# Three feed-forward steps summed pair by pair during the attention, window masks in strided selections, some early loads on ScalarE's queue, and a new order

## The chip, the core and the metric

The kernel runs on one core of a Trainium2 chip. A core has five engines with their own instruction queues: TensorE (PE in the profile, with PEld for its weight loads), VectorE (DVE), ScalarE (ACT), GpSimd (POOL) and SyncE (SP), which here only issues loads and stores. The engines meet through semaphores. The metric is the time of one execution on the device in microseconds (us), lower is better.

## The reference, cut to what matters

Eight batches, eight heads, 512 local and 32 global tokens, head size 64. Local queries see the 32 globals and a band of 32 tokens to either side; global queries see everything. The concatenated heads of all 4352 rows then go through a feed-forward block without bias.

```python
s_ll = np.where(np.abs(pos[:, None] - pos[None, :]) <= 32, s_ll, -1000000000.0)
out_l = np.matmul(sm(np.concatenate([s_lg, s_ll], axis=-1)), np.concatenate([v_g, v_l], axis=2))
out_g = np.matmul(sm(s_g), v_all)
x = np.ascontiguousarray(attn_out.transpose(0, 2, 1, 3)).reshape(B * S, H * D)
h = x @ w_in            # 4352 x 512 by 512 x 2048
return ((h - np.tanh(h)) @ w_out).astype(np.float32)
```

## The kernel before, in words

Everything is written as operations (class `Order`): each has a function that issues its instructions, the engines that may do it with their costs, the keys that it reads and writes, a due time, and for TensorE the PSUM banks that it needs. When the kernel is built, `Order.run` plays them through as a list schedule and writes the instructions of each engine in the order that comes out. The tables `CFG`, `NUDGE`, `CHOICE` and `HOLD` are the numbers that shift due times, engine preferences and starts, so they alone set the order; on the chip each engine then works its list strictly from front to back.

The work has three stretches. First, batch 0's attention in four head pairs (class `Pair`): transposes of keys and queries, scores, softmax (smallest value on VectorE, exponential on ScalarE, normalising on GpSimd), transposes of the probabilities, and the product with the values (L824). In this stretch TensorE has gaps, which are filled with matmuls on a mask that nobody reads (`fill`, L1943). Meanwhile the weights arrive as 64-bit numbers, of which the load brings all bytes; ScalarE (`rebias`, L525), VectorE (`low` L529, `join` L533) make them float32, and they are split into a high part (`high`, L446) and a remainder (`rest`, L539, on GpSimd). The activations x are split likewise into x_hi and x_lo (L446, L835).

Second, for batches 1 to 7 attention in windows (class `WindowPair`), between which TensorE does the feed-forward block of the batch before (class `Chunk`): 16 steps, each with a sum h of 12 matmuls of 512 columns (three products high-high, high-low, low-high times four blocks of d_model, one block per head pair, L1290), then tanh on ScalarE (L1298), h - tanh on VectorE (L1301), its high part ghi (L446) and remainder glo (L1307), and 12 matmuls with w_out into four accumulator banks (L1338). A step's sum can begin only when all four head pairs of the batch are done, since `add_hidden` takes one product over all four blocks as one operation. `add_window_masks` writes the masks of the windows on GpSimd, block by block. Third, the tail: the last batch's feed-forward block with combined products (L1660, L1686, L1780).

The first pair of the windows is interleaved with the end of batch 0's attention: its scores (L960, L976) and the smallest values of its windows on VectorE (L1053, "window peaks" below) come before x of the last head pair is finished. All loads but two are issued by SyncE.

## Time and profile before

| | |
|---|---|
| time, median of 3 runs | 906.06 us (904.59 to 906.87) |
| the profiled execution | 903.53 us, its span 901.6 us |
| TensorE busy | 883.5 us, 98% of the span |
| VectorE, ScalarE, GpSimd busy | 643.9, 405.9, 319.9 us |
| granted TensorE clock | 0.999 of full speed, the 2.4 GHz level |
| first and last matmul | 5.23 us, 897 us |

Read it with two cautions. Busy time of TensorE is from start to modelled end of pipelined matmuls, so 98% says that it is hardly ever without work, not that it is at its peak. And the average hides that the first 65 us are another regime than the rest, which is why the rows below come from stretches.

### The profile page before, as it was taken

The numbers are of one execution on the slowest core, as the hardware profiler recorded it, in microseconds if no ns is written. First come the engines' busy times: TensorE is split into PE (matmuls) and PEld (weight loads), VectorE is DVE, ScalarE is ACT, GpSimd is POOL, SyncE is SP. The second block draws the span as 40 slices with busy tenths as digits, with TensorE's granted clock in tenths as the row PEclk, the third lists the DMA queues.
The fourth block names the chain that finished last, engine by engine and source line by source line (L and its number), as shares of the span: only waits on it lengthen the run. The fifth ranks groups of instructions, "written<-read, shape, count | busy, mean of one in ns | idle before, by whom it ended". The sixth has DMA issues, their size and how long they took to land.

```text
span 901.6 us, 21546 instructions
## 1 busy us (share of the span) xinstructions
PE 883.5 (98%) x7664; PEld 730.2 (81%) x7664; DVE 643.9 (71%) x2309; ACT 405.9 (45%) x1192; POOL 319.9 (35%) x525
## 2 busy tenths in 40 slices
PE   6889999999999999999999999999999999999998
PEld 4668888888888888888888888888888888899886
DVE  6997767877777557857777557857777658787662
ACT  6986665534344334423444343423444343443332
POOL 7767765333333323333333323323333323000000
PEclk9999999999999999999999999999999999999999
DMA  9768746533334223423334223423334110100001
GB/s 224 173 182 221 185 104 139 124 72 65 66 65 113 45 54 67 96 61 64 66 65 113 46 51 73 95 61 62 65 70 108 43 31 13 47 0 1 1 1 71
DMA packets 266059, 72.20 MB, mean 80 GB/s; under 512 B 250593, under 2 KB 259297, under 8 KB 265953
## 3 DMA queue, kind: packets, MB, share of 16 engines
q1 hardware_dynamic: 264752, 70.44, 34.5%
q8 instruction: 61, 1.00, 0.4%
q10 hardware_dynamic: 1200, 0.39, 0.2%
q14 instruction: 46, 0.37, 0.1%
HBM read 61.87 MB, written 8.91 MB: 79 GB/s over the span
## 4 chain that ended last, share of the span: by engine, by line
PE 91%; DVE 2%; DMA 2%; ACT 1%; POOL 1%; SPq 1%; issue 1%; POOLq 0%; ACTq 0%; DVEq 0%
PE bank L1338 34%; PE bank L1290 32%; PE bank L1660 7%; PE bank L1147 6%; PE bank L1780 6%; PE bank L960 3%; PE bank L976 1%; PE bank L1686 1%; DVE keys_first L1092 1%; DMA stage<-in_moe_w_out_dram 1%; DMA values<-in_v_g_dram 0%; DMA wpair<-in_moe_w_out_dram 0%; ACT prob L1237 0%; ACT t L1237 0%; DMA first_q<-in_moe_w_in_dram 0%
## 5 line engine op out<-in xcount | busy, mean ns | idle before, releaser
L1307 POOL TENSOR_TENSOR glo<-t,ghi 128x512 fp32r<-128x512 f32 x112 | 146.1, 1304 | 291.3 <-PE bank L1338 233.5
L1092 DVE STREAM_TRANSPOSE keys_first<-prob 32x256 f32<-32x256 f32 x384 | 167.3, 436 | 10.6 <-POOL prob L1074 3.5
L1298 ACT ACTIVATE t<-bank 128x512 f32<-128x512 f32 x112 | 66.7, 596 | 179.7 <-PE bank L1290 175.9
L1301 DVE TENSOR_TENSOR t<-bank,t 128x512 f32<-128x512 f32 x112 | 76.6, 684 | 80.0 <-ACT t L1298 78.4
L1338 PE MATMUL bank<-w_out_lo,ghi 128*128 128x512 f32 x448 | 124.9, 393 | 0.0
L1338 PE MATMUL bank<-w_out_hi,ghi 128*128 128x512 f32 x448 | 124.1, 391 | 0.4 <-ACT ghi L446 0.4
L1338 PE MATMUL bank<-w_out_hi,glo 128*128 128x512 f32 x448 | 124.2, 391 | 0.0
L1290 PE MATMUL bank<-x_lo,w_in_hi 128*128 128x512 f32 x448 | 120.2, 390 | 1.3 <-DVE x_lo L835 1.3
L1290 PE MATMUL bank<-x_hi,w_in_hi 128*128 128x512 f32 x448 | 120.8, 392 | 0.4 <-ACT x_hi L446 0.4
L446 ACT CAST ghi<-t 128x512 fp32r<-128x512 f32 (+1 forms) x118 | 72.5, 614 | 107.3 <-PE bank L1338 82.7
L1290 PE MATMUL bank<-x_hi,w_in_lo 128*128 128x512 f32 x448 | 119.8, 389 | 0.0
L1074 POOL TENSOR_SCALAR prob<-prob,st 128x128 f32<-128x128 f32 x224 | 80.6, 378 | 109.0 <-DVE st L456 79.5
L1053 DVE CUSTOM_DVE_ANT_0 prob<-bank,wraw 128x128 f32<-128x128 f32 x224 | 53.7, 287 | 82.3 <-PE bank L960 81.5
L1290 PEld LDWEIGHTS bank<-x_lo,w_in_hi 128*128 128x128 f32 x448 | 84.1, 188 | 19.3 <-DVE x_lo L835 1.7
L1338 PEld LDWEIGHTS bank<-w_out_hi,ghi 128*128 128x128 f32 x448 | 83.9, 188 | 19.6 <-issue 1.8
L1338 PEld LDWEIGHTS bank<-w_out_lo,ghi 128*128 128x128 f32 x448 | 83.0, 188 | 20.4 <-issue 4.0
L1290 PEld LDWEIGHTS bank<-x_hi,w_in_hi 128*128 128x128 f32 x448 | 83.3, 188 | 19.6 <-DVE st L1053 1.2
L1338 PEld LDWEIGHTS bank<-w_out_hi,glo 128*128 128x128 f32 x448 | 83.5, 188 | 19.4 <-issue 2.4
L1290 PEld LDWEIGHTS bank<-x_hi,w_in_lo 128*128 128x128 f32 x448 | 84.1, 188 | 17.6
L1061 ACT ACTIVATE prob<-prob,st 128x128 f32<-128x128 f32 x224 | 87.9, 401 | 1.0 <-DVE st L1053 0.2
L446 ACT CAST x_hi<-bank 128x256 fp32r<-128x256 f32 x62 | 20.6, 375 | 86.1 <-PE bank L976 84.3
L1147 PEld LDWEIGHTS bank<-keys_first,values 128*64 128x64 f32 x784 | 49.3, 138 | 10.3 <-DVE t L1301 5.6
(230 smaller groups left out, 1373.4 us busy)
## 6 DMA issues: line engine op xcount, KB each, us to landing
rawkq<-in_q_l_dram SPq DMA_DIRECT2D x112, 64.0 KB, 2.2
rawkq<-in_k_l_dram SPq DMA_DIRECT2D x112, 64.0 KB, 2.4
out_dram<-wpair SPq DMA_DIRECT2D x28, 256.0 KB, 2.3
values<-in_v_l_dram SPq DMA_DIRECT2D x28, 120.0 KB, 2.3
keys_first<-in_v_l_dram SPq DMA_DIRECT2D x28, 120.0 KB, 2.7
stage<-in_moe_w_out_dram SPq DMA_DIRECT2D x6, 512.0 KB, 4.4
wpair<-in_moe_w_out_dram SPq DMA_DIRECT2D x6, 512.0 KB, 5.4
first_q<-in_moe_w_in_dram SPq DMA_DIRECT2D x6, 512.0 KB, 4.8
```

Source lines behind the costliest of these rows:

```text
L446: (nc.scalar.copy if e == "A" else nc.vector.tensor_copy)(dst, src)
L1061: nc.scalar.activation(x, x, AF.Exp, bias=s[:, k:k + 1], scale=-1.0, accum_out=s[:, 8 + k:9 + k])
L1074: nc.gpsimd.tensor_scalar(x, x, s[:, k:k + 1], 1.0, op0=ALU.mult, op1=ALU.mult)
L1092: nc.vector.transpose(view(win_kf[W * k:W * k + W], [(CH, 2), (P, NT), (1, W)], 3 * G + W * i), src)
L1147: nc.tensor.matmul(dst, win_values[h][:, window(b)], src, start=n == 0, stop=n == len(parts) - 1, skip_group_check=True)
L1290: nc.tensor.matmul(self.h[s][:, j * n:(j + 1) * n], w[:, cc, f * P:(f + 1) * P], self.x()[xi][:, cc, :n], start=part == 0 and cc == 0 and ...
L1298: nc.scalar.activation(tt_[q], self.h[s], AF.Tanh)
L1301: nc.vector.tensor_sub(tt_[q], self.h.pop(s), tt_[q])
L1307: eng[e].tensor_sub(gg[q][1], tt_[q], f32(gg[q][0]))
L1338: nc.tensor.matmul(self.acc[tt], g[:, j * self.n + tt * P:j * self.n + (tt + 1) * P], low_out(f) if wi else high_out(f), start=s == 0 and ...
L1660: nc.tensor.matmul(self.hold(tt, tags), g(), low_out(f) if wi else high_out(f), start=first and k < len(tts), stop=last and k == len(mms) - 1)
L1780: nc.tensor.matmul(dst[:, at], w, m, start=fresh and n == 1, stop=n == 6, skip_group_check=True)
```

## The change

Three things in the code, and the tables that set the order.

The first three steps of batch 0's feed-forward block (`AHEAD = 3`) no longer have their sum as three operations over all four blocks of d_model but as four operations over one block each (`column`: three matmuls). A block's operation reads only the x of its own head pair. The first two of these sums sit in banks of the accumulator pool. The window masks come in two operations of strided selections over up to five blocks at once instead of four with one selection per block. And loads of weights, of the raw keys and queries after the first pair, and of batch 0's values may be issued by SyncE or ScalarE, whichever the list schedule finds earlier with a penalty. `CFG`, `NUDGE`, `CHOICE` and `HOLD` are new throughout; of the tables a few lines stand for all.

```diff
@@ -297,6 +297,7 @@
+    AHEAD = 3
...
-    CFG = dict(win=1940.613, a_g=0.0342, a_kg=0.1721, a_ph=0.0237, a_qs=1.4715, a_w=0.0254, a_wn=0.1779, a_xg=7.3446, d_g=0.274,
+    CFG = dict(win=-1646.8252, a_g=0.121, a_kg=0.1264, a_ph=0.1183, a_qs=3.1154, a_w=0.0917, a_wn=0.0597, a_xg=7.3446, d_g=82.3869,
...
@@ -454,6 +465,12 @@
     def add_epsilon(x, to, y):
         nc.vector.tensor_reduce(out=y, in_=view(x, [(1, x.shape[1]), (to, 2)]), axis=mybir.AxisListType.X, op=ALU.add)
         nc.vector.reciprocal(x, y)
+
+    def queue(e):
+        return nc.scalar if e == "A" else nc.sync
+
+    def queues(d):
+        return [("S", d), ("A", d + 0.15, CFG["a_ld"])]

     def either(n, kind, psum=False):

@@ -515,7 +532,7 @@
         def load(e, _):
             if WIDE:
                 box["v"] = raw[:, :, 0]
-                nc.sync.dma_start(raw.bitcast(I32).rearrange("p (a c) k -> p a (c k)", a=a), src)
+                queue(e).dma_start(raw.bitcast(I32).rearrange("p (a c) k -> p a (c k)", a=a), src)
             else:
                 box["v"] = raw.rearrange("p n k -> p (n k)")[:, :N]
                 nc.sync.dma_start(box["v"].rearrange("p (a c) -> p a c", a=a), src)
@@ -539,7 +556,7 @@
             eng[e].tensor_sub(lo(), box["v"].rearrange("p (a c) -> p a c", a=a), f32(hi()))

         own = [("w", kind, f, i, p) for i in ((j,) if half else (0, 1)) for p in range(2)]
-        add(("S", 0.37), load, due, w=keys, res=spare, xfer=0.9 * N / 256)
+        add(queues(0.37), load, due, w=keys, res=spare, xfer=0.9 * N / 256)
         if WIDE:
             add(("A", (N + 300) / 1200), rebias, due, r=keys, w=keys)
             add(("D", (N / 2 + 146) / 960), low, due, r=keys, w=keys, lock=True)
@@ -614,12 +631,12 @@
             def load(a, src):
                 def fn(e, _):
                     for h in range(2):
-                        (nc.scalar if h and self.j == 0 else nc.sync).dma_start(first_raw[self.set][:, a, :, h],
+                        (nc.scalar if h and self.j == 0 else queue(e)).dma_start(first_raw[self.set][:, a, :, h],
                                                                              src[self.b, 2 * self.jj + h].rearrange("(t p) d -> p t d", p=P))
                 return fn

             for a in range(2):
-                add(("S", 0.95), load(a, (k_l, q_l)[a]), self.due(self.C["o_ld"] - 8), w=[self.key[a]], xfer=1.3)
+                add(queues(0.95) if self.j else ("S", 0.95), load(a, (k_l, q_l)[a]), self.due(self.C["o_ld"] - 8), w=[self.key[a]], xfer=1.3)

         def add_turn(self):
             rk, rq, pw, pk, pq = self.key
@@ -854,22 +871,23 @@
         return k + k // 3

     def add_window_masks():
-        def mask(j):
+        def blocks(i, c, n, step):
+            return view(win_m()[W * i:W * i + W], [(step, n), (1, W)], c)
+
+        places = {-1: ((0, P, 3, P), (1, 0, 4, P), (2, 0, 4, P), (3, 0, 3, P), (3, 3 * P + W, 1, P)),
+                  1: ((0, W, 3, 160), (0, 480, 1, P), (1, 64, 2, 160), (1, 352, 2, 96), (2, 96, 2, P), (2, 320, 2, 160), (3, 96, 1, P), (3, 192, 2, 160))}
+
+        def mask(s):
             def fn(e, _):
-                m = win_mask(j)
-                nc.gpsimd.memset(m, 0.0)
-                for i in range(4):
-                    rows, b = slice(W * i, W * i + W), 4 * j + i
-                    for n in range(3):
-                        k = window(b) + n
-                        c = W * (pos(k) - pos(window(b)))
-                        x = m[rows, c:c + W]
-                        if abs(k - b) > 1:
-                            nc.gpsimd.memset(x, BIG)
-                        elif k != b:
-                            s = k - b
-                            nc.gpsimd.affine_select(out=x, in_=x, pattern=[[-s, W]], base=0, channel_multiplier=s,
-                                                    compare_op=ALU.is_ge, fill=BIG)
+                if s < 0:
+                    nc.gpsimd.memset(win_m()[:, :S], 0.0)
+                for p in places[s]:
+                    x = blocks(*p)
+                    nc.gpsimd.affine_select(out=x, in_=x, pattern=[[0, p[2]], [-s, W]], base=0, channel_multiplier=s,
+                                            compare_op=ALU.is_ge, fill=BIG)
+                if s > 0:
+                    nc.gpsimd.memset(win_m()[:W, 2 * W:3 * W], BIG)
+                    nc.gpsimd.memset(win_m()[3 * W:, 3 * P:3 * P + W], BIG)
             return fn

         def ends(e, _):
@@ -878,8 +896,8 @@
                 nc.vector.memset(win_gmask()[W * rows:W * rows + W, W * lo:W * hi], BIG)

         due = base(H) - 300
-        for j in range(NT):
-            add(("P", 1.85), mask(j), due + j, w=["gm"], )
+        for x in (-1, 1):
+            add(("P", 2.15), mask(x), due + x, w=["gm"])
         add(("D", 0.77), ends, due, w=["gm"])

     def add_globals(b):
@@ -1249,11 +1267,11 @@

                 src = v_l[self.b, self.h]
                 for a in range(2):
-                    nc.sync.dma_start(raw[:96, 3 * a:3 * a + 3], bass.AP(src.tensor, src.offset + 224 * D * a, [[D, 96], [96 * D, 3], [1, D]]))
+                    queue(e).dma_start(raw[:96, 3 * a:3 * a + 3], bass.AP(src.tensor, src.offset + 224 * D * a, [[D, 96], [96 * D, 3], [1, D]]))
                 g = v_g[self.b, self.h]
-                nc.sync.dma_start(raw[96:], bass.AP(g.tensor, g.offset, [[D, G], [0, 6], [1, D]]))
-
-            add(("S", 1.45), load, self.pair.due(self.C["o_vl"] + self.C["o_tw"] * self.two), w=[f"vh{self.two}"], xfer=0.95)
+                queue(e).dma_start(raw[96:], bass.AP(g.tensor, g.offset, [[D, G], [0, 6], [1, D]]))
+
+            add(queues(1.45), load, self.pair.due(self.C["o_vl"] + self.C["o_tw"] * self.two), w=[f"vh{self.two}"], xfer=0.95)


     step_no = [0]
@@ -1308,7 +1326,23 @@

             self.g[s] = gg[q]
             fs = range(s * self.per, (s + 1) * self.per)
-            for part in range(3):
+            early = s < AHEAD and self.name == "b0"
+
+            def column(cc):
+                def fn(e, tags):
+                    if cc == 0:
+                        self.h[s] = bank([P, 512], tags[hk])
+                    for wi, xi in ((0, 0), (0, 1), (1, 0)):
+                        nc.tensor.matmul(self.h[s], (w_in_hi, w_in_lo)[wi][:, cc, s * P:(s + 1) * P], self.x()[xi][:, cc, :n],
+                                         start=cc == 0 and wi + xi == 0, stop=cc == NCC - 1 and wi == 1)
+                return fn
+
+            for cc in range(NCC * early):
+                r = [k + (xi,) for k in self.xkeys if k[2] // 2 == cc for xi in range(2)] + [("w", "i", s, j, wi) for j in range(2) for wi in range(2)]
+                last = cc == NCC - 1
+                add(("T", 0.68), column(cc), due + 0.1 * cc - CFG["ahead"] * (not last), r=r, w=[hk],
+                    res=[tk] if last else (), alloc=[(hk, "acc" if s < 2 else "h")] if cc == 0 else ())
+            for part in range(3 * (not early)):
                 wi, xi = ((0, 0), (0, 1), (1, 0))[part]
                 r = [k + (xi,) for k in self.xkeys] + [("w", "i", f, j, wi) for f in fs for j in range(2)]
                 add(("T", 0.907), mm(part), due + 0.1 * part, r=r, w=[hk],
```

What stands in the engines' lists shows it best. In the rows below a line number is that of the kernel before or of the changed kernel, `bank_96` to `bank_103` are the eight PSUM banks, and xN means that a row stands N times.

TensorE, before: behind batch 0's last product with the values the fillers come, of which the first row here is the last, then the sums of steps 0 and 1 (24 matmuls), then the transposes of the first windows (the first shown), and after those the first w_out products (L1338).

```order
L1943 MATMUL bank_96<-mask_88 128x224
L1290 MATMUL bank_96<-x_hi_85,w_in_hi 128x512 x4
L1290 MATMUL bank_99<-x_hi_85,w_in_hi 128x512 x4
L1290 MATMUL bank_99<-x_lo_86,w_in_hi 128x512 x4
L1290 MATMUL bank_99<-x_hi_85,w_in_lo 128x512 x4
L1290 MATMUL bank_96<-x_lo_86,w_in_hi 128x512 x4
L1290 MATMUL bank_96<-x_hi_85,w_in_lo 128x512 x4
L1114 MATMUL bank_98<-idr,prob 128x64
```

TensorE, changed, the same place from the second half of that last product on: L1336 is a `column`, one block of one step.

```order
L841 MATMUL bank_102<-keys_first,values 64x128 x2
L841 MATMUL bank_102<-keys_first,values 64x64 x2
L841 MATMUL bank_102<-keys_first,values 64x160 x2
L1336 MATMUL bank_96<-x_hi_85,w_in_hi 128x512
L1336 MATMUL bank_96<-x_lo_86,w_in_hi 128x512
L1336 MATMUL bank_96<-x_hi_85,w_in_lo 128x512
L1336 MATMUL bank_100<-x_hi_85,w_in_hi 128x512
L1336 MATMUL bank_100<-x_lo_86,w_in_hi 128x512
L1336 MATMUL bank_100<-x_hi_85,w_in_lo 128x512
L1336 MATMUL bank_103<-x_hi_85,w_in_hi 128x512
L1336 MATMUL bank_103<-x_lo_86,w_in_hi 128x512
L1336 MATMUL bank_103<-x_hi_85,w_in_lo 128x512
```

What moved: 27 of the 36 matmuls of steps 0 to 2 need only x of the first three pairs and stand between the products and transposes of the attention from the second pair on (the last three of them are the first three L1336 here); 9 need the last pair's x, of which the 6 here come before the window transposes and the first w_out products (L1372), and 3 of step 2 behind the first eight of those. The sums of steps 1 and 0 lie in `bank_100` and `bank_103`, which the w_out products take over as accumulators. Before the first w_out product stand 33 matmuls of feed-forward sums instead of 24, and 69 fillers instead of 78. Behind it the numbers of matmuls are equal in each kind, apart from these 9.

VectorE, before, behind the first window peaks (L1053, the row ahead of these); the next rows are the two x_lo of the last pair (L835).

```order
L450 TENSOR_REDUCE st_91<-st_91 32x2 x3
L533 SCALAR_TENSOR_TENSOR stage<-stage 128x512
L455 TENSOR_REDUCE st_91<-st_91 128x4
L456 RECIPROCAL st_91<-st_91 128x4
L533 SCALAR_TENSOR_TENSOR first_kw_63<-first_kw_63 128x256
L1005 TENSOR_REDUCE st_91<-st_91 32x2
L940 STREAM_TRANSPOSE hi_104<-rawkq 128x512
L455 TENSOR_REDUCE st_91<-st_91 128x4
L456 RECIPROCAL st_91<-st_91 128x4
L933 STREAM_TRANSPOSE first_m<-rawkq 128x5x96
L934 STREAM_TRANSPOSE first_m<-rawkq 128x32
L450 TENSOR_REDUCE st_91<-st_91 32x2 x3
```

VectorE, changed, the same place: the last window peaks (L1071) stand ahead, L852 is x_lo.

```order
L461 TENSOR_REDUCE st_91<-st_91 32x2 x3
L466 TENSOR_REDUCE st_91<-st_91 128x4
L467 RECIPROCAL st_91<-st_91 128x4
L1023 TENSOR_REDUCE st_91<-st_91 32x2
L546 TENSOR_SCALAR stage<-stage 128x512
L958 STREAM_TRANSPOSE hi_104<-rawkq 128x512
L852 TENSOR_TENSOR x_lo_86<-bank_101,x_hi_85 128x256
L856 COPY xg<-bank_101 128x32
L466 TENSOR_REDUCE st_91<-st_91 128x4
L467 RECIPROCAL st_91<-st_91 128x4
L461 TENSOR_REDUCE st_91<-st_91 32x2 x3
L852 TENSOR_TENSOR x_lo_86<-bank_102,x_hi_85 128x256
```

What moved: the transposes into `first_m` now stand among the peaks, and two `join` operations on weights, one of 512 and one of 256 columns, are gone from between the peaks and x_lo: the smaller stands earlier, the larger weight's comes later. From the first window peak to the second x_lo the lists have else the same instructions. In the stretch up to the first window peak VectorE has six more: one more w_out_hi cast, one more x_hi cast, two more copies of `first_g`, two more `join` of 256 columns, one more `low` of 256 and one fewer of 512; a 512-column copy of `first_q` less and one of `keys_first` more cancel.

ScalarE, before, from its start (L446 is a copy, L525 `rebias`, L676 and L677 the global exponentials).

```order
L617 DMA first_raw<-in_k_l_dram 128x4x64
L617 DMA first_raw<-in_q_l_dram 128x4x64
L446 ACT_TABLE_LOAD
L446 COPY first_g<-bank_96 128x128
L446 COPY first_m<-bank_96 64x4x32 x2
L446 COPY first_kw<-first_g 128x2x2x32
L446 COPY first_kw<-bank_97 128x2x96
L446 COPY first_kw<-bank_97 128x2x192
L446 COPY first_kw<-first_g 128x2x2x32
L525 ACTIVATE stage<-stage 128x512
L676 ACTIVATE pg<-pg,st_91 64x32
L677 ACTIVATE pg,st_91<-pg,st_91 64x576
```

ScalarE, changed, from its start (L1255 is the exponential of a window of scores).

```order
L634 DMA first_raw<-in_k_l_dram 128x4x64
L634 DMA first_raw<-in_q_l_dram 128x4x64
L535 DMA stage<-in_moe_w_out_dram 128x1024
L634 DMA first_raw<-in_k_l_dram 128x4x64 x2
L457 ACT_TABLE_LOAD
L457 COPY first_g<-bank_96 128x128
L457 COPY first_m<-bank_96 64x4x32 x2
L457 COPY first_kw<-first_g 128x2x2x32
L1270 DMA values<-in_v_l_dram 96x3x64 x2
L1272 DMA values<-in_v_g_dram 32x6x64
L1255 ACTIVATE t_68,st_91<-t_68,st_91 128x224 x2
L1255 ACTIVATE prob,st_91<-prob,st_91 128x224 x2
```

What moved: six of the first stretch's loads go from SyncE to ScalarE, three at its start and three ahead of its first exponential, each of these three behind a semaphore of an earlier load; the first `rebias` goes behind the first eight exponentials. Eight more loads, of weights, stand on ScalarE behind the first w_out product, most behind a semaphore of GpSimd, which has to be done with the buffer. On GpSimd the two instructions of the identity now stand ahead of the three of one of the first masks, and the window masks are 13 selections and 3 fills instead of 30 and 6.

## Rows read from the trace of the kernel before

**Rows 1.** The page: busy time and share of the span of each engine.

```profile
PE 883.5 (98%) x7664; PEld 730.2 (81%) x7664; DVE 643.9 (71%) x2309; ACT 405.9 (45%) x1192; POOL 319.9 (35%) x525
```

**Rows 2.** Stretches (start:end length, busy us and instructions of each engine, clock, DMA share, GB/s).

```profile
5.23:52.70 47.47, 41.38 (x507) 30.85 (x507) 41.47 (x168) 42.14 (x137) 34.04 (x82) 1.00 0.87 207
52.70:65.48 12.78, 10.34 (x87) 8.01 (x88) 12.32 (x57) 9.86 (x34) 8.89 (x13) 1.00 0.67 179
65.48:897.40 831.92, 831.74 (x7070) 691.37 (x7070) 588.82 (x2073) 352.29 (x1023) 272.85 (x412) 1.00 0.31 70
```

**Rows 3.** Timeline of TensorE: start, length, what [idle before <- releaser].

```profile
5.23 0.68 PE L579 MATMUL bank<-idr,first_kw 64*128 64x64 f32 x4 [5.23 <-DVE idr L1384]
...
55.05 1.61 PE L1943 MATMUL bank<-mask 128*128 128x224 bf16 x15
...
65.48 1.20 PE L1338 MATMUL bank<-w_out_hi,ghi 128*128 128x512 f32 x4 [0.38 <-ACT ghi L446]
...
68.33 1.07 PE L1338 MATMUL bank<-w_out_hi,glo 128*128 128x512 f32 x4
```

**Rows 4.** Chain that ended last, in order of time: start, length, what.

```profile
31.66 4.47 DMA values<-in_v_g_dram
...
64.17 0.61 DVE t L1301
...
64.81 0.63 ACT ghi L446
```

**Rows 5.** Timeline of VectorE at the end of the first attention.

```profile
52.70 0.28 DVE L1053 CUSTOM_DVE_ANT_0 prob<-bank,wraw 128x128 f32<-128x128 f32 x1
...
59.03 1.36 DVE L529 TENSOR_SCALAR stage<-stage 128x512 int32<-128x512 int32 x1
...
60.74 0.41 DVE L835 TENSOR_TENSOR x_lo<-bank,x_hi 128x256 fp32r<-128x256 f32 x1
...
64.10 0.67 DVE L1301 TENSOR_TENSOR t<-bank,t 128x512 f32<-128x512 f32 x1
```

**Rows 6.** VectorE by line and form, 5 to 66 us: busy, mean ns.

```profile
L533 DVE SCALAR_TENSOR_TENSOR stage<-stage 128x512 int32<-128x512 int32 x6 | 4.0, 668 | 0.0
L529 DVE TENSOR_SCALAR first_q<-first_q 128x512 int32<-128x512 int32 x3 | 1.2, 410 | 0.0
L446 DVE CAST x_hi<-bank 128x256 fp32r<-128x256 f32 x2 | 0.8, 412 | 0.0
L533 DVE SCALAR_TENSOR_TENSOR first_kw<-first_kw 128x256 int32<-128x256 int32 x1 | 0.4, 395 | 0.0
L529 DVE TENSOR_SCALAR first_kw<-first_kw 128x256 int32<-128x256 int32 x1 | 0.3, 283 | 0.0
```

**Rows 7.** ScalarE by line and form, 5 to 66 us.

```profile
L1298 ACT ACTIVATE t<-bank 128x512 f32<-128x512 f32 x2 | 1.2, 596 | 1.0 <-PE bank L1290 1.0
L446 ACT CAST ghi<-t 128x512 fp32r<-128x512 f32 x1 | 0.6, 618 | 0.9 <-DVE t L1301 0.9
```

**Rows 8.** Timeline of GpSimd: a mask of the first kind, the identity, window masks.

```profile
3.24 0.28 POOL L1392 MEMSET mask<- 128x224 bf16 x1
...
4.30 0.20 POOL masks.py:197 MEMSET pg<- 128x128 f32 x1
...
8.04 1.60 POOL L871 TENSOR_SCALAR_AFFINE_SELECT wraw<-wraw 32x32 bf16<-32x32 bf16 x8
```

**Rows 9.** What TensorE waited for, 0 to 66 us: total, times, longest.

```profile
PE bank L824 <- DMA values<-in_v_g_dram: 2.3, 4, 1.2
```

**Rows 10.** An issue on SyncE's queue (timeline: start, length).

```profile
4.92 0.50 SPq L518 DMA_DIRECT2D stage<-in_moe_w_out_dram  x1
```

**Rows 11.** GpSimd's third w_in remainder, from the chain.

```profile
52.78 1.30 POOL w_in_lo L539
```

**Rows 12.** The DMA engines in 10 to 15 us (columns as in rows 2).

```profile
10.00:15.00 5.00, 4.19 (x41) 3.66 (x40) 4.22 (x27) 4.90 (x17) 4.08 (x18) 1.00 1.17 287
```

**Rows 13.** DMA issues: count, KB each, median us to landing.

```profile
wpair<-in_moe_w_out_dram SPq DMA_DIRECT2D x6, 512.0 KB, 5.4
```

39 lines of the change are left out of this document (20 added, 19 removed), and 141 rows, old and new, of tables (CHOICE, HOLD, NUDGE).

## Prediction

> **What bounds the kernel now.** I read the page first: TensorE is busy for 98% of the span, every other engine for 71% at most [rows 1]. An average says little where stages differ, so I cut the span at the first w_out product (65.48 us) and at the first window peak on VectorE (52.70 us) [rows 2]. From 65.48 to 897.40 us TensorE is busy for 831.74 of 831.92 us: it waits for nobody, and the time there is the number of matmuls. Four 512-column matmuls stand at 0.91 us (68.33 to 69.24 us in the timeline, of which the row at 68.33 is shown [rows 3]; the chain has 8 in 2.11 with the first one's fill), 0.227 each, at a granted clock of 1.00. Before 52.70 us it is another regime: VectorE is busy for 41.47 and ScalarE for 42.14 of 47.47 us, TensorE for 41.38, but part of TensorE's work is filler, such as the 15 matmuls at 55.05 us [rows 2, 3]. So until 52.70 us VectorE and ScalarE set the pace. The chain of waits shows what joins the two: through a load of v_g at 31.66 us, and at the end through VectorE's h - tanh, ScalarE's ghi and the first w_out product [rows 4].
>
> Two questions follow. How many matmuls are left when the saturated stretch begins, and when does it begin?
>
> **The matmuls moved.** Ahead of the first w_out product stand 33 matmuls of feed-forward sums instead of 24. The nine that are gone from the saturated stretch are worth 9 x 0.227 = 2.0 us. The 27 that need only three pairs lie in gaps of TensorE; the cover is there, since 69 fillers remain of 78, and fillers are written only into gaps. Without cover each triple would hold the attention for 0.7 us.
>
> **From the first window peak to the first w_out product: 12.78 us before** [rows 2]. VectorE goes from the first peak at 52.70 to the end of the second x_lo at 60.74 + 0.41 = 61.15 us, 8.45 us with hardly a gap [rows 5]. The changed list has the same instructions there less a `join` of 512 columns (0.668) and one of 256 (0.395) [rows 6]: 7.39 us. One `low` of 512 columns took 1.36 us here where the others of its form take 0.41 [rows 5, 6], and it stays in the list; I leave it at 1.36, which keeps a possible gain of 0.95 out. Behind x_lo TensorE has five matmuls that need it, 5 x 0.227 plus 0.4 for the last to come out: 1.55. Then tanh 0.60, h - tanh 0.67, ghi 0.62 [rows 5, 7], and some 0.2 of semaphores: 3.65 us, where before it was 65.48 - 61.15 = 4.33. VectorE has about 2 us of other work in that time (one `join`, one `low`, one cast) and is done with it before tanh is. The accumulators need the banks of steps 1 and 0; the second h - tanh, 0.67 behind the first, ends as ghi does, so it costs nothing unless it slips. Together 7.39 + 3.65 = 11.05 instead of 12.78: 1.7 us earlier. Bounds: 0.7 earlier if the peaks, with the transposes now between them, hold up ScalarE's exponentials by 1 us; 2.7 if the 1.36 falls to 0.41.
>
> **The start of the window peaks.** VectorE's list is longer up to there: a w_out cast (no row of that form; the 256-column x_hi cast, 0.41, is the nearest), an x_hi cast 0.41, two copies of 128 columns (at most that each; I take 0.3), two joins of 0.395, a `low` of 256 at 0.283, less one of 512 at 0.41 [rows 6]. That is 2.1 us. VectorE was idle for 6.0 us of the 47.47 [rows 2], some of which this fills; I take 1.6. Against it stand two things. TensorE's first matmul waits until 5.23 us for the identity [rows 3], which GpSimd wrote from 4.30 us; its two instructions now stand ahead of three that took from 3.24 to 4.30 [rows 8], 1.06 us. The transposes behind it need loads that are only just there, so I take 0.6 of that. And TensorE waited four times for v_g, 2.3 us in all [rows 9]. Six early loads leave SyncE's queue, where an issue takes 0.50 [rows 10], so that what stands behind comes 3 us earlier; but the chain passes only one of these four waits, and the queue also waits for buffers, so 0.5. Sum: 1.6 - 0.6 - 0.5 = 0.5 us later. Bounds: 2.1 later if nothing is hidden and nothing won; 2.3 earlier if VectorE's work all goes into idle time (0), the start gives 1.06, and the longest v_g wait, 1.2, goes.
>
> **At nothing:** the issues on ScalarE ahead of its first exponential (0.5 each, while it waited in the profile for TensorE and for a weight), and the window masks. GpSimd took 1.60 us for eight selections [rows 8] and now has 13 wider ones instead of 30 small. VectorE's last fills of these masks have moved ahead of its first score peaks and wait for GpSimd; a mask end that is late there would cost up to 0.5 us. The feed-forward stretch as a whole stands at nothing, since its matmuls are the same ones and TensorE had 0.18 us of idle time in it.
>
> **Sum:** -2.0 - 1.7 + 0.5 = -3.2 us. Against the profiled execution's 903.53 that is 900.3; its 901.6 us span and the 1.9 around it are kept. The profiled execution lies 2.5 below the median of the three runs, so against that median, which is what a measurement will give, I forecast 906.06 - 3.2 = 902.8 us, -0.36%. About 0.3%, 2.7 us, is what a measurement of this kernel can tell from no change.
>
> **Rivals.**
>
> *The loads gain nothing.* In 10 to 15 us the DMA engines' mean share is 1.17 at 287 GB/s [rows 12], which is to say full: a load that is issued earlier then only makes the others later. SyncE's issues would be saved, the landings not, and the early 512 KB of w_out on ScalarE's queue would compete with the queries that the first transposes need. Then start and v_g give nothing and the peaks begin 1.6 to 2.1 later: -2.0 - 1.7 + 1.9 = -1.8, 904.3 us. Against it: over the whole first stretch the gaps are there, and the queue itself was held by its buffers, not by the engines alone. The Trainium skill's page "DMA: Bandwidth & Descriptors", section "Issuing engines are not separate DMA queues", says just this: loads from several engines run on the same 16 DMA engines, and issuing from more than one saves only the time of issuing. By that rule, the sum is this rival's, and the share of 1.17 agrees with it for the first 20 us.
>
> *The early sums stall.* TensorE works in order; a column whose weights are late holds the attention behind it. Before, GpSimd finished the third w_in remainder at 52.78 + 1.30 = 54.08 us [rows 11]. Step 2's first column now stands just ahead of the last half of the last product, which began at about 54 us before. If its weights come no earlier than before and the product comes 2 us earlier, the wait is up to 2 us: -3.2 + 2 = -1.2, 904.9 us. For it: GpSimd takes 1.30 for each remainder. Against it: the changed list places that remainder ahead of the first window normalising, with two half pieces before it, and GpSimd was idle for 13 of the first 47 us [rows 2].
>
> *It goes better.* Every bound falls to the good side: -2.0 - 2.7 - 2.3 = -7.0, 899.1 us; half of it beyond the forecast is 901.
>
> *Slower: ScalarE stands at a load.* Eight weight loads now stand in ScalarE's list in the feed-forward stretch, most behind GpSimd's release of the buffer or an earlier load's landing. A load of 512 KB takes 5.4 us to landing [rows 13]; behind it stand tanh and ghi, and TensorE needs a ghi every 24 x 0.227 = 5.4 us. ScalarE is busy for 352 of 832 us there [rows 2], so one stand is swallowed or costs 2 to 3 us; it decides from a sum of 6 us on, which takes two or three full stands that all reach TensorE: 906.06 - 3.2 + 6 = 908.9 us.
>
> **How the numbers follow.** Forecast 0.48, with its own range 901.3 to 904.3: 0.40 below the bound for faster (903.3), 0.08 above. Loads gain nothing 0.18, early sums stall 0.12: both within 0.3%, with 0.04 that fall below. Better 0.14, faster. Slower 0.08, of which 0.02 stays within. So faster 0.40 + 0.04 + 0.14 = 0.58, slower 0.06 and 0.02 for a mishap that I have not seen: 0.08, same 0.34. The range of 8 in 10 leaves out the outer half of "better" and the slower case: 899.8 to 906.5.
>
> **What would show it.** In the profile after: the first w_out product at 65.48 - 1.7 + 0.5 = 64.3 us, 33 matmuls of sums ahead of it; TensorE without waits behind it; the first window peak at 53.2; x_lo 7.4 behind it; the first matmul at 4.2 to 4.6 us; fewer waits for v_g. The prediction is wrong if window peaks begin after 55 us, if TensorE waits for w_in_lo before 60 us, or if it waits for ghi or ScalarE for a load between 65 and 140 us.

## The result: 917.4 us, 1.2% slower

The changed kernel takes 917.39 us (median of 4, 916.68 to 917.54), the kernel before beside it on the same chip 906.23 (median of 4, 904.59 to 906.87): ratio 1.0127, 95% interval 1.0115 to 1.014, 11.2 us more. The forecast was 902.8 with a range to 906.5. The profiled execution took 917.53 with a span of 915.7; that of before lies 2.5 below its own median, so between the two traces it is 14.1 us that have to be found.

The page and the same stretches, cut again at the first window peak and the first w_out product (answers [rows 1, 2]; columns as there), and below them two windows of 10 us:

```profile
PE 888.2 (97%) x7655; PEld 731.8 (80%) x7655; DVE 667.6 (73%) x2358; ACT 393.3 (43%) x1140; POOL 327.1 (36%) x508
```

```profile
5.23:59.48 54.25, 46.17 (x516) 33.21 (x516) 44.32 (x170) 41.56 (x136) 35.09 (x64) 1.00 0.79 187
59.48:70.08 10.60, 8.44 (x83) 5.74 (x75) 9.28 (x45) 8.58 (x31) 7.91 (x12) 1.00 0.77 199
70.08:912.00 841.92, 832.95 (x7061) 692.38 (x7061) 612.22 (x2128) 342.05 (x975) 279.98 (x415) 1.00 0.31 70
100.00:110.00 10.00, 9.04 (x33) 7.30 (x34) 7.21 (x28) 7.55 (x26) 7.74 (x11) 0.83 0.71 186
170.00:180.00 10.00, 6.42 (x95) 4.75 (x73) 6.44 (x40) 5.50 (x22) 2.16 (x5) 0.83 0.52 118
```

Three readings. The window peaks start at 59.48 instead of 52.70, 6.8 us later. From there to the first w_out product it is 10.60 us instead of 12.78, 2.2 less. And the stretch that had 0.18 us without work now has 9: from the first w_out product to the end of the last matmul it is 841.4 us (70.08 to 911.52) where it was 831.9 (65.48 to 897.35), although nine matmuls fewer stand in it. 4.6 us are lost ahead of the first w_out product and 9.5 behind it.

What TensorE waited for behind it, in total (us, times, longest; the row left out is the wait that ends with the first w_out product itself):

```profile
PE bank L1308 <- DVE st L1071: 3.5, 1, 3.5
PE bank L1372 <- ACT w_out_hi L457: 3.3, 1, 3.3
PE bank L978 <- DVE t L1319: 1.4, 2, 0.8
...
PE bank L1372 <- POOL w_out_lo L556: 0.3, 1, 0.3
```

Timeline of TensorE in the changed kernel (answers [rows 3]):

```profile
4.22 0.66 PE L596 MATMUL bank<-idr,first_kw 64*128 64x64 f32 x4 [4.22 <-DVE idr L1418]
8.48 1.95 PE L650 MATMUL bank<-idr,first_raw 128*128 128x128 f32 x8 [3.60 <-DMA first_raw<-in_k_l_dram]
...
70.08 1.20 PE L1372 MATMUL bank<-w_out_hi,ghi 128*128 128x512 f32 x4 [0.80 <-ACT ghi L457]
...
100.96 2.00 PE L1308 MATMUL bank<-x_hi,w_in_hi 128*128 128x512 f32 x4 [3.49 <-DVE st L1071]
102.76 1.88 PE L1308 MATMUL bank<-x_lo,w_in_hi 128*128 128x512 f32 x4
104.47 1.12 PE L1308 MATMUL bank<-x_hi,w_in_lo 128*128 128x512 f32 x4
...
174.45 0.49 PE L1372 MATMUL bank<-w_out_hi,ghi 128*128 128x512 f32 x1 [3.25 <-ACT w_out_hi L457]
```

It stands twice, until 100.96 and until 174.45 us. Four 512-column matmuls begin 0.91 us apart at full clock; behind the first stand they begin 1.80 and 1.71 apart, twice as far. The granted clock in the window 100 to 110 is 0.83: 3.4 of 10 us at the lower level, 1.2 instead of 2.4 GHz, after 3.5 us without a matmul; the window with the second stand reads the same. So each of these two stands costs itself and some 1.7 us more (estimate: 3.4 us at half the speed). The sum: 8.5 of waits, 2 x 1.7 of clock, less 2.0 for nine matmuls is 9.9, measured 9.5.

What were the engines named there waiting for? VectorE and ScalarE in the changed kernel, around both stands:

```profile
59.48 0.29 DVE L1071 CUSTOM_DVE_ANT_0 prob<-bank,wraw 128x128 f32<-128x128 f32 x1 [1.95 <-PE bank L978]
...
87.54 1.53 DVE L546 TENSOR_SCALAR wpair<-wpair 128x512 int32<-128x512 int32 x1 [4.19 <-DMA wpair<-in_moe_w_out_dram]
...
94.23 1.53 DVE L546 TENSOR_SCALAR stage<-stage 128x512 int32<-128x512 int32 x1
95.87 1.62 DVE L550 SCALAR_TENSOR_TENSOR stage<-stage 128x512 int32<-128x512 int32 x1
97.41 0.28 DVE L1071 CUSTOM_DVE_ANT_0 prob<-bank,wraw 128x128 f32<-128x128 f32 x1
...
173.06 0.29 DVE L546 TENSOR_SCALAR wpair<-wpair 128x256 int32<-128x256 int32 x1 [6.42 <-DMA wpair<-in_moe_w_out_dram]
```

```profile
1.79 0.53 ACTq L535 DMA_DIRECT2D stage<-in_moe_w_out_dram  x1
...
86.18 0.67 ACT L542 ACTIVATE first_q<-first_q 128x512 f32<-128x512 f32 x1 [6.62 <-DMA first_q<-in_moe_w_in_dram]
...
173.05 0.44 ACT L542 ACTIVATE wpair<-wpair 128x256 f32<-128x256 f32 x1 [5.56 <-DMA wpair<-in_moe_w_out_dram]
```

The window peaks for which TensorE waits at 97 to 101 us begin at 97.41, behind three conversions of 1.4 to 1.6 us, which are behind 4.19 us in which VectorE stood at a weight that had not landed; ScalarE stood 6.62 us at another. At the second stand it is one weight of 256 KB, at which VectorE stood 6.42 and ScalarE 5.56 us, with the next window peaks and the cast of w_out_hi behind it. All of these loads were issued by SyncE. Its queue and GpSimd's releases of the two buffers:

```profile
1.67 0.45 SPq L634 DMA_DIRECT2D first_raw<-in_k_l_dram  x1
...
14.00 2.28 SPq L634 DMA_DIRECT2D first_raw<-in_q_l_dram  x2
...
65.75 1.47 SPq L1217 DMA_DIRECT2D values<-in_v_l_dram  x1
...
79.48 2.14 SPq L947 DMA_DIRECT2D rawkq<-in_q_l_dram  x4
81.72 0.43 SPq L535 DMA_DIRECT2D first_q<-in_moe_w_in_dram  x1
82.25 0.45 SPq L535 DMA_DIRECT2D wpair<-in_moe_w_out_dram  x1
...
164.81 2.14 SPq L947 DMA_DIRECT2D rawkq<-in_k_l_dram  x4
167.04 2.02 SPq L947 DMA_DIRECT2D rawkq<-in_q_l_dram  x4
169.17 0.44 SPq L535 DMA_DIRECT2D wpair<-in_moe_w_out_dram  x1
```

```profile
73.13 1.77 POOL L556 TENSOR_TENSOR w_in_lo<-first_q,w_in_hi 128x512 fp32r<-128x512 f32 x1
74.86 1.50 POOL L556 TENSOR_TENSOR w_out_lo<-wpair,w_out_hi 128x512 fp32r<-128x512 f32 x1
```

The buffer of first_q is free at 74.9 us and that of wpair at 76.4, but their loads are issued at 81.72 and 82.25: ahead of them on SyncE's list stand sixteen loads of window values (from 65.75 to 79.4) and the raw queries. The 256 KB load at 169.17 stands behind eight raw loads. SyncE in the kernel before:

```profile
6.99 0.93 SPq L617 DMA_DIRECT2D first_raw<-in_k_l_dram  x2
...
55.87 0.33 SPq L1199 DMA_DIRECT2D values<-in_v_l_dram  x1
...
66.99 0.55 SPq L518 DMA_DIRECT2D stage<-in_moe_w_out_dram  x1
...
82.90 0.34 SPq L518 DMA_DIRECT2D wpair<-in_moe_w_out_dram  x1
...
153.11 1.02 SPq L518 DMA_DIRECT2D wpair<-in_moe_w_out_dram  x2
```

There the window values began ten microseconds earlier, eight weight loads followed from 66.99 to 82.90, and the last two of all were issued from 153.11.

At the start the changed kernel's first key transposes wait until 8.48 us (5.84 before) for a load issued at 1.67, as before, that now takes 6.7 us to landing instead of 3.7: ScalarE issues 512 KB of w_out at 1.79 us, right behind it, which SyncE issued at 4.92 before [rows 10]. The raw keys and queries of the third pair (pair 2, counted from 0), issued from 6.99 us before, now come from 14.00 on, behind three more weight loads and the values.

### The profile page after: what moved, and what is told of

Same layout as the page of the kernel before. It is cut to its first block, busy times and chain, and to the rows that moved or that the text cites. A ratio compares the mean times of both kernels' runs of the same rounds, so it can differ in the third digit from the quotient of the medians.

```text
span 915.7 us, 21498 instructions
## 1 busy us (share of the span) xinstructions
PE 888.2 (97%) x7655; PEld 731.8 (80%) x7655; DVE 667.6 (73%) x2358; ACT 393.3 (43%) x1140; POOL 327.1 (36%) x508
## 4 chain that ended last, share of the span: by engine, by line
PE 89%; DMA 3%; DVE 3%; ACT 2%; SPq 1%; issue 1%; POOL 1%; DVEq 0%; POOLq 0%; ACTq 0%
PE bank L1372 33%; PE bank L1308 32%; PE bank L1694 7%; PE bank L1814 6%; PE bank L1165 5%; PE bank L978 3%; DMA first_q<-in_moe_w_in_dram 1%; PE bank L1720 1%; PE bank L994 1%; DMA first_raw<-in_k_l_dram 1%; DMA stage<-in_moe_w_out_dram 1%; SPq L947 1%; PE bank L1336 0%; DMA wpair<-in_moe_w_out_dram 0%; DVE t L1248 0%
## 5 line engine op out<-in xcount | busy, mean ns | idle before, releaser
L457 ACT CAST ghi<-t 128x512 fp32r<-128x512 f32 (+1 forms) x122 | 74.7, 613 | 125.6 <-PE bank L1372 87.9
L1372 PE MATMUL bank<-w_out_hi,ghi 128*128 128x512 f32 x448 | 123.8, 391 | 4.1 <-ACT w_out_hi L457 3.3
L1372 PE MATMUL bank<-w_out_lo,ghi 128*128 128x512 f32 x448 | 125.8, 395 | 0.3 <-POOL w_out_lo L556 0.3
L1372 PE MATMUL bank<-w_out_hi,glo 128*128 128x512 f32 x448 | 124.3, 392 | 0.0
L1308 PE MATMUL bank<-x_hi,w_in_hi 128*128 128x512 f32 x436 | 118.7, 394 | 3.5 <-DVE st L1071 3.5
L1308 PE MATMUL bank<-x_lo,w_in_hi 128*128 128x512 f32 x436 | 117.9, 393 | 0.0
L1308 PE MATMUL bank<-x_hi,w_in_lo 128*128 128x512 f32 x436 | 116.6, 389 | 0.0
L1071 DVE CUSTOM_DVE_ANT_0 prob<-bank,wraw 128x128 f32<-128x128 f32 x224 | 53.8, 287 | 81.5 <-PE bank L978 80.6
L1372 PEld LDWEIGHTS bank<-w_out_hi,ghi 128*128 128x128 f32 x448 | 83.8, 188 | 22.7 <-ACT w_out_hi L457 3.6
L1372 PEld LDWEIGHTS bank<-w_out_lo,ghi 128*128 128x128 f32 x448 | 82.6, 188 | 22.3 <-issue 5.5
L1372 PEld LDWEIGHTS bank<-w_out_hi,glo 128*128 128x128 f32 x448 | 83.6, 188 | 18.8 <-issue 1.8
L1308 PEld LDWEIGHTS bank<-x_hi,w_in_lo 128*128 128x128 f32 x436 | 82.0, 188 | 17.2
L1165 PE MATMUL bank<-keys_first 128*64 128x32 f32 (+2 forms) x784 | 54.6, 228 | 0.0
```

The costliest lines, as they stand in the source:

```text
L457: (nc.scalar.copy if e == "A" else nc.vector.tensor_copy)(dst, src)
L1165: nc.tensor.matmul(dst, win_values[h][:, window(b)], src, start=n == 0, stop=n == len(parts) - 1, skip_group_check=True)
L1308: nc.tensor.matmul(self.h[s][:, j * n:(j + 1) * n], w[:, cc, f * P:(f + 1) * P], self.x()[xi][:, cc, :n], start=part == 0 and cc == 0 and ...
L1372: nc.tensor.matmul(self.acc[tt], g[:, j * self.n + tt * P:j * self.n + (tt + 1) * P], low_out(f) if wi else high_out(f), start=s == 0 and ...
```

## The experiments

Each kernel is the changed one with instructions moved or one line altered. Every time is a median beside runs of the kernel before on the same chip, every ratio is to that. The intervals reach some 0.2% to either side, so 2 us between two of these kernels lie within them. Theory A: the places of a few loads in SyncE's list cost the time. B: the loads that ScalarE issues cost it. C: the early columns cost it, since they stand on TensorE ahead of attention that has to be early.

**All loads on SyncE, at the same places of the list.**

```diff
-        return nc.scalar if e == "A" else nc.sync
+        return nc.sync
```

> The changed kernel, with every load that ScalarE's queue may issue put back on SyncE's queue at the same place of the program; nothing else differs. The changed kernel took 917.4 us. Theory A (the places of a few loads are at fault, not the engine that issues them): the 512 KB of w_out is issued a little later than at 1.79 us, so the first key transposes start 1 to 2 us earlier than at 8.48, and both stalls of TensorE (91 to 101 and 171 to 175 us) stay: 914 to 917. Theory B (issuing from ScalarE is at fault, its waits and the second queue): both stalls and the late start go: 903 to 907. Theory C (the early column sums hold TensorE): no change, 917.

919.99 us, ratio 1.0142 (1.012 to 1.0165): no gain, so B falls as the cause of the 11 us. The first exponential is at 11.33 us (14.38 in the changed kernel) and SyncE waits for landed loads 3.1 us in the first 180 instead of 22.1, but the peaks come at 58.59 and TensorE waits 4.4 us for w_in_hi, 2.4 for VectorE. At these places of the list it does not help that SyncE issues; what the places themselves are worth, the next runs show.

**The first w_out back on SyncE alone; then all first loads in their old places.** The second also puts pair 2's raw loads ahead of the third and fourth weight, and the values on SyncE. SyncE's list in the second:

```diff
 L634 DMA first_raw<-in_q_l_dram 128x4x64 x3
+L535 DMA stage<-in_moe_w_out_dram 128x1024
+L535 DMA wpair<-in_moe_w_out_dram 128x1024
+L634 DMA first_raw<-in_k_l_dram 128x4x64 x2
 L535 DMA first_q<-in_moe_w_in_dram 128x4x256
-L535 DMA wpair<-in_moe_w_out_dram 128x1024
+L634 DMA first_raw<-in_q_l_dram 128x4x64 x2
+L1270 DMA values<-in_v_l_dram 96x3x64 x2
...
 L535 DMA stage<-in_moe_w_in_dram 128x4x256
...
-L634 DMA first_raw<-in_q_l_dram 128x4x64 x2
-L634 DMA first_raw<-in_k_l_dram 128x4x64 x4
+L634 DMA first_raw<-in_k_l_dram 128x4x64 x2
```

> The changed kernel, with one load moved: the 512 KB of w_out that ScalarE issues at 1.79 us is issued by SyncE behind the raw keys and queries of the first two pairs, as before the change. Theory A: the key transposes start at about 5.9 instead of 8.48 us, first exponentials and first w_out product 2.6 us earlier, the stalls later on stay as they are: 914.8. If the stall at 91 to 101 us is only the late start passed on through the buffers: 908 to 910. Theory C (column sums): window peaks stay near 59 us whatever the start does: 917.

> The changed kernel, with the first loads in the places that they had before the change: the 512 KB of w_out and the values of batch 0 on SyncE's queue, and the raw keys and queries of the third pair ahead of the third and fourth weight load instead of behind them and behind the values. Theory A (places of loads): they are issued at 7 to 10 instead of 14.0 to 15.5 us, ScalarE doesn't stand at a values load, and the first window peak comes at about 56.5 instead of 59.48; with both later stalls unchanged 914.5, and with the stall at 91 to 101 us gone too, because the buffers come free earlier, 909. Theory C (column sums hold TensorE and with it the window scores): the peak stays near 59, 917.

The first alone: 917.22 us, 1.0115 (1.0086 to 1.0144), nothing. The transposes start at 5.97, as before the change, but ScalarE then stands where it issues the values itself:

```profile
12.14 0.48 ACT L1255 ACTIVATE t<-t,st 128x224 f32<-128x224 f32 x1 [6.04 <-DMA values<-in_v_l_dram]
```

The second: 915.59, 1.010 (1.0078 to 1.0122), first peak at 57.19, first w_out product at 67.80, 2.3 earlier; the waits near 100 and 172 us stay. By the trace the start costs some 2 us of the 11; the time alone, 1.8 less, lies within the intervals.

**The early columns gathered ahead of each step's last column, where they no longer stand in the attention.** On TensorE, nine times:

```diff
 L841 MATMUL bank_102<-keys_first,values 64x160 x2
-L1336 MATMUL bank_103<-x_hi_85,w_in_hi 128x512
-L1336 MATMUL bank_103<-x_lo_86,w_in_hi 128x512
-L1336 MATMUL bank_103<-x_hi_85,w_in_lo 128x512
 L720 MATMUL bank_97<-idr,pg 128x64 x6
```

> The changed kernel, with the early columns taken out of the early places: the 27 matmuls of the first three columns of three steps stand, in the same order, directly ahead of the step's last column. Theory A (the columns fill gaps and are worth their length): the first window peak comes up to 1.95 us earlier, and 27 x 0.227 = 6.1 us of matmuls are then on the path: 917.4 + 4 = 921.5. Theory C (they hold the window scores): 914 to 915.

920.86, 1.0153 (1.0135 to 1.0171): the first peak 0.9 earlier, the first w_out product 0.8 later, the time longer. C falls as the cause of the 11 us: moved out of the attention, the columns cost more than they did in it. The price of their place alone is not shown by this time, since nine of the 27 matmuls now stand behind the first w_out product (2.0 us) and the mean granted clock is 0.990 instead of 0.995; the peaks put it at 0.9 us.

**One conversion of w_out behind the next window peaks.** VectorE's `low` and `join` of one weight, ScalarE's cast and GpSimd's remainder with them, and behind the cast the next weight load into the same buffer, which ScalarE issues.

```diff
-L546 TENSOR_SCALAR stage<-stage 128x512
-L550 SCALAR_TENSOR_TENSOR stage<-stage 128x512
 L1071 ISA prob,st_92<-bank_97,wraw_172 128x128
...
+L546 TENSOR_SCALAR stage<-stage 128x512
+L550 SCALAR_TENSOR_TENSOR stage<-stage 128x512
 L951 STREAM_TRANSPOSE first_m<-rawkq 128x5x96
```

> The changed kernel, with one weight conversion (the two VectorE instructions of w_out's step 8, then its cast and remainder) put behind the window peaks of the second step at 97 us instead of ahead of them. Theory A: the peaks begin 3.1 us earlier, TensorE's wait of 3.49 us at 97.5 to 101 falls to under 1 and the half clock behind it (1.7) goes: 917.4 - 4.8 = 912.6. Rival: the weights of a later step are then late in its place and TensorE waits for them: 916 to 918.

920.76, 1.0158 (1.0143 to 1.0174). The wait for the peaks falls to 1.7 us, but TensorE's waits in this kernel name others:

```profile
PE bank L1132 <- POOL prob L1092: 1.9, 2, 1.5
PE bank L1308 <- DVE st L1071: 1.7, 1, 1.7
```

Behind the first w_out product the waits add up to 7.9 us where they were 8.5, so moving the conversion has mostly moved the wait. That the time is 3.4 us longer is not a matter of these waits: the mean granted clock is 0.992 instead of 0.995, and some of the difference lies in a place that the edit does not touch (last section). That a conversion ahead of the peaks is where lateness shows, not where it comes from, this run suggests and the next ones show.

**The weight loads of 80 us.** The first kernel puts the two loads that were issued at 81.72 and 82.25 ahead of the sixteen window values, and the third weight ahead of the raw queries. The second leaves the values ahead of the weights and takes the raw keys and queries of the windows' third pair from ahead of both:

```diff
 L535 DMA stage<-in_moe_w_in_dram 128x4x256
-L947 DMA rawkq<-in_k_l_dram 32x16x32 x4
 L1217 DMA values<-in_v_l_dram 96x5x64
...
 L1220 DMA keys_first<-in_v_l_dram 64x4x64
-L947 DMA rawkq<-in_q_l_dram 32x16x32 x4
 L535 DMA first_q<-in_moe_w_in_dram 128x4x256
 L535 DMA wpair<-in_moe_w_out_dram 128x1024
+L947 DMA rawkq<-in_k_l_dram 32x16x32 x4
 L535 DMA stage<-in_moe_w_in_dram 128x4x256
+L947 DMA rawkq<-in_q_l_dram 32x16x32 x4
 L535 DMA stage<-in_moe_w_out_dram 128x1024
```

> The changed kernel, with SyncE's queue reordered at 65 to 83 us: two weight loads (one of w_in, one of w_out) go ahead of the 16 issues of window values, a third ahead of the four issues of raw queries. Theory A: they are issued at about 75, 76 and 80 to 85 us instead of 81.7 to 82.8, so VectorE's wait of 4.19 us at 83.3 goes, and with it most of TensorE's waits of 1.42 and 3.49 us at 91 to 101 and some 1.8 of half clock: 917.4 - 6 = 911 us; up to 2 us of it lost if the values, now later, hold the first window product. Theory C (column sums) or a bound of VectorE by its own work: 916 to 918.

> The changed kernel with the raw keys and queries of the windows' third pair (eight issues on SyncE, 3.4 and 2.1 us) moved from ahead of and behind the sixteen loads of window values to behind the two, and the third, weight loads that follow. Theory A, the stall at 91 to 101 us comes from weight loads that stand in SyncE's list behind other loads while their buffers are free (first_q and wpair issued 81.7 and 82.3, buffers free at 74.9 and 76.4): they are issued 4 to 5 us earlier, the waits for w_in_hi, w_out_hi and VectorE's st near 100 us fall from 4.9 to under 2 us and the half clock behind them goes: 917.4 - 3 to 6 = 911.4 to 914.4 us. Rival, the loads are late because the conversions ahead of them are late and the queue's place does not matter: the waits stay within 1 us of 4.9 and the time is 916.5 to 918.5, or the raw keys are now what is missing and a wait for their transposes takes the place: 917 to 921.

The first: 920.28, 1.015 (1.0127 to 1.0172). The two loads are issued at 75.97 and 77.44, but the values behind them push the third weight from 82.79 to 88.26, and TensorE's waits from 91 to 102 us stay, at 5.2 us where they were 4.9: 1.3 for VectorE's t, 1.1 for ghi, 2.8 for VectorE's st. The second: 913.0, 1.008 (1.0052 to 1.0108), 4.4 less than the changed kernel. All weights come earlier, the first two as soon as their buffers are free:

```profile
75.48 0.62 SPq L535 DMA_DIRECT2D first_q<-in_moe_w_in_dram  x1
77.15 0.35 SPq L535 DMA_DIRECT2D wpair<-in_moe_w_out_dram  x1
```

VectorE no longer stands there, and TensorE waits for no peak; 1.8 us for w_in_hi are left, until 116.71, and the second stand, 2.8 us for w_out_hi until 170.70. Behind that one the clock stays at 1.00 (last section), so some 1.7 of the 4.4 us come from a place that this edit does not touch.

**The last weight load ahead of the eight raw loads.**

```diff
 L1220 DMA keys_first<-in_v_l_dram 64x4x64
-L947 DMA rawkq<-in_k_l_dram 32x16x32 x4
-L947 DMA rawkq<-in_q_l_dram 32x16x32 x4
 L535 DMA wpair<-in_moe_w_out_dram 128x512
+L947 DMA rawkq<-in_k_l_dram 32x16x32 x4
+L947 DMA rawkq<-in_q_l_dram 32x16x32 x4
```

> The changed kernel, with one load moved on SyncE's queue: the last 256 KB of w_out is issued ahead of eight issues of raw keys and queries instead of behind them. Theory A: it is issued at about 164.8 instead of 169.17 us and lands at about 168.7 instead of 173.0, so VectorE's conversion no longer stands there for 6.4 us with the window peaks behind it; the waits of 3.25 + 0.33 us go, and the half clock behind them, some 1.8: 917.4 - 5.4 = 912.0. Rival (VectorE or GpSimd is late there anyway, or the raw keys and queries are now late in its place): 916 to 918.

912.28 (911.46 to 913.01, 5 runs), 1.0062 (1.0039 to 1.0084), 5.1 less. The window in which the changed kernel had 6.42 us of work at 0.83:

```profile
170.00:180.00 10.00, 10.00 (x136) 8.22 (x134) 8.29 (x45) 7.67 (x28) 4.13 (x10) 1.00 0.49 102
```

3.6 us of waiting went, and with it the lower clock, 1.00 for 0.83 in this window. The other 1.5 us of the gain agree with the 1.7 reckoned for it, though such a difference of two medians is no finer than their intervals.

**Together.** First loads, last load and the conversion behind the peaks; the first two alone; those two with the move of the raw keys and queries.

> Three edits together: the first loads in their old places, the second step's window peaks ahead of one weight conversion, and the last 256 KB of w_out ahead of eight raw loads (which alone gave 912.28). Theory A: the gains add up, 917.4 - 5.1 - 4.8 - 2.9 = 904.6. Rival (each stall that goes uncovers the next): 908 to 911.

> The changed kernel with two edits that have each been measured alone: the first loads in their old places (alone 1.8 us less than the changed kernel) and the last load of w_out ahead of the eight raw loads (alone 5.1 us less). Theory A, the two are separate places and their waits add: 917.4 - 1.8 - 5.1 = 910.5 us (909.5 to 912), first window peak near 57.2, no wait of TensorE at 171 to 175 us, the waits near 100 us (VectorE's st, ScalarE's w_out_hi or w_in_hi) as large as with the first edit alone. Rival, the stall is only passed on: 912 to 915, with a wait of over 2 us somewhere behind 105 us.

> All three moves of loads at once. Theory A: 910.5 - 3 to 6 = 904.5 to 907.5 us, that is, as the kernel before, with a first window peak still 4.5 us later than in it, made good by nine matmuls fewer and the shorter way from the peak to the first w_out product. Rival (the stall near 100 us stays or moves): 910 to 913.

912.54, 1.0063 (1.0046 to 1.008): no better than the last load alone, and, with the interval of the next one, not clearly worse than without the conversion's move. 911.76, 1.006 (1.0038 to 1.0082): 5.6 less than the changed kernel where 6.9 were expected; in its trace the first peak is at 59.27, not at 57.2, with 1.38 us ahead of it in which VectorE waited for GpSimd's w_in_lo, so the first loads' gain did not show in that execution (the three other kernels with these loads have it at 56.87, 57.19 and 57.76). And 905.67 (10 runs), 1.0 (0.9984 to 1.0017): the three moves of loads, which touch no instruction that computes, take the 11.2 us back. The first of them also hands four loads from ScalarE to SyncE; the weight loads behind the first w_out product are still ScalarE's, so those are not the cause. Singly the moves were worth 1.8, 5.1 and 4.4, together 11.3 against 11.7 measured, each with about 2 us of uncertainty.

**Two more stands.** In the last kernel's trace ScalarE stands at a load with a cast behind it that TensorE wants, and VectorE at window scores that stand on TensorE behind two early columns:

```profile
PE bank L1308 <- ACT w_in_hi L457: 1.7, 1, 1.7
```

```profile
113.65 0.68 ACT L542 ACTIVATE stage<-stage 128x512 f32<-128x512 f32 x1 [3.25 <-DMA stage<-in_moe_w_in_dram]
```

```profile
57.76 0.29 DVE L1071 CUSTOM_DVE_ANT_0 prob<-bank,wraw 128x128 f32<-128x128 f32 x1 [1.95 <-PE bank L978]
```

The cast goes ahead of the conversion, and the scores ahead of the two columns:

```diff
-L542 ACTIVATE stage<-stage 128x512
 L457 CAST w_in_hi<-first_q 128x4x128
+L542 ACTIVATE stage<-stage 128x512
```

> All three moves of loads and two more places where an engine stands ahead of what TensorE wants. On ScalarE the cast of w_in_hi stands behind the conversion of the next weight, which waits 3.25 us for its load at 110.4 to 113.65 us, and TensorE waits 1.7 us for that cast: the cast goes ahead. On TensorE the scores of the first windows stand behind two early column operations, and VectorE waits 1.95 us for them at 57.76: the scores go ahead, the columns behind the product that follows. Theory A (each wait on the path is worth its length): no wait for w_in_hi behind 100 us, first window peak 1 to 1.5 us earlier (56.3 to 56.8), first w_out product at 67: 905.7 - 1.7 - 1.4 = 902.6 us (901.5 to 904), against the kernel before -0.4% (-0.5 to -0.2). Rival, the waits are only handed on (the columns are missing from the gap they filled, the next weight comes later by the cast): 904.5 to 907.

903.78 (903.26 to 904.6, 7 runs), ratio 0.9973 (0.9962 to 0.9984): 0.3% faster than the kernel before and 1.5% faster than the changed one, inside its forecast. The peaks start at 56.27, 1.5 earlier, as expected, though the first w_out product comes at 67.91, not 67: of the 1.5 it gains 0.5. All that TensorE waits for behind 60 us in this kernel:

```profile
PE bank L1372 <- ACT ghi L457: 0.8, 1, 0.8
PE bank L1336 <- DVE x_lo L852: 0.6, 1, 0.6
PE bank L1308 <- POOL w_in_lo L556: 0.5, 1, 0.5
PE bank L1308 <- DVE st L1071: 0.4, 1, 0.4
PE bank L1308 <- ACT w_in_hi L457: 0.3, 1, 0.3
```

## Why the prediction was wrong

**Matmuls moved (-2.0): right.** 33 sum matmuls stand ahead of the first w_out product. In the best kernel, where the stands are gone, it is 830.6 us from that product (67.91) to the end of the last matmul (898.55), 1.2 less than before, with 1.2 us of waits left.

**From the first peak to the first w_out product (-1.7): right,** -2.2 measured, inside its bounds (-0.7 to -2.7), though its two parts were both off and partly cancel. From the first peak to the end of the second x_lo it is 6.50 us, not 7.39: the `low` of 1.36 takes 0.41 here, the gain that the prediction had left out. From there to the first w_out product it is 4.10, not 3.65: ScalarE does two conversions and an exponential ahead of tanh, which begins 1.6 us after x_lo.

**The start of the peaks (+0.5): the sign held, the size failed,** +6.8. Two of its parts were wrong. It took 0.6 and 0.5 us off for the earlier identity and for loads that leave SyncE's queue. The identity did come (first matmul 4.22 instead of 5.23), but the first score peak on VectorE stands at 13.95 instead of 10.97 (in the changed kernel, then before):

```profile
13.95 0.39 DVE L1248 CUSTOM_DVE_ANT_0 t<-bank,mask 128x224 f32<-128x224 f32 x1
```

```profile
10.97 0.39 DVE L1230 CUSTOM_DVE_ANT_0 t<-bank,mask 128x224 f32<-128x224 f32 x1 [0.53 <-PE bank L728]
```

That is 3.0 later, 2.6 of it since the transposes wait for raw keys that share the first microseconds with 512 KB more (with that load moved they start at 5.97). VectorE's added work was 2.1 us, as reckoned (41.30 us busy from 13.95 to 59.48; 39.17 from 10.97 to 52.70), but no idle time swallowed it: VectorE is idle 1.7 us longer there than before, and 1.95 us of its idle time are one wait, at the first peak, for window scores that TensorE does behind early columns. 3.0 + 2.1 + 1.7 is the 6.8. The rival that the loads gain nothing had the mechanism, that the early 512 KB compete with what the first transposes need, and priced it at a gain lost, not at 2.6 us more. The Trainium skill's page "DMA: Bandwidth & Descriptors", section "Issuing engines are not separate DMA queues", says that loads run on the same 16 DMA engines whichever engine issues them, and that a second issuer saves only the time of issuing. The run with all loads on SyncE agrees as far as it goes: with one issuer the kernel takes 919.99 us, 2.6 more than with two, at intervals that overlap.

**At nothing, the feed-forward stretch: this is the step that failed.** It was costed by its matmuls and by the 0.18 us of idle time before, and priced its loads only as issues on ScalarE. +11.5 us of waits and clock came from there (9.5 measured plus the 2.0 won). The prediction had a rival for a stand at a load, at 908.9 with a chance of 0.08: two or three stands that reach TensorE. That came true in kind, the sum that it asked for was passed, and two of the prediction's own signs against it came: peaks after 55 us, and ScalarE at a load (6.62 us until 86.18). But it looked at ScalarE, for loads that ScalarE issues; the stands were VectorE's and ScalarE's conversions of weights that SyncE issued late. Of SyncE's queue the prediction priced six loads that leave it at the start; what is behind what in it after 60 us had no term, nor a bound. Together -2.0 - 2.2 + 6.8 + 11.5 = 14.1 us, the difference of the two traces.

**The early sums stall: no.** TensorE never waited for w_in_lo there. **Window masks at nothing: nearly right.** GpSimd had them at 10.2 us (13.8 before) and was idle until 18.49. VectorE's fills of them stand from 13.15 to 13.92, directly ahead of the first score peak, which comes 1.43 us after TensorE begins the scores, where it was 1.18: 0.25 us, inside the 0.5 allowed for.

What stays open: why the changed kernel's peaks are still 3.6 us later in the best version than before (56.27 and 52.70). VectorE's 2.1 us of added work is part of it; the rest was not tried apart.

## What to carry to other kernels

When an order is new, read the list of the queue that issues the loads as closely as those of the engines that compute, all the way to its last load: a load that is issued some 6 us after its buffer is free, behind loads that nobody wants yet, is a wait to come. A conversion that stands in an in-order engine ahead of what TensorE needs passes a late load on. Moving one conversion here moved the wait (8.5 us became 7.9); moving the loads took it away. Price a stand of TensorE of three microseconds at one and a half times its length where the trace shows the clock fall behind it, which it did not behind every one, and check it by a run.
